# A new order of attention steps, and a PSUM tile of its own for each pair's product, in a fused fp32 attention and two-layer MLP kernel

## The chip, the core and the metric

The kernel runs on one core of a Trainium2 chip. The metric is the device time of one execution in microseconds (us); the time of a kernel is the median of several executions. Five engines work side by side, each through its own queue in order: PE (TensorE, matrix products), DVE (VectorE), ACT (ScalarE), POOL (GpSimd) and SP (SyncE, which here issues all transfers and a few relays).

## What is computed

Causal attention over 2 batches of 12 heads, 448 positions and 64 columns per head; its output, read as 896 tokens of 768 columns, goes through two blocks of two matrix products each.

```python
# attention, q, k, v of shape (2, 12, 448, 64)
scores = np.where(mask, -1e9, q @ k.T / 8)          # mask: keys later than the query
attn = exp(scores - max) / sum                      # softmax per query
x = (attn @ v), heads side by side                  # (896, 768)
# first block: 768 -> 2048 -> 768
h = x @ w_in;  x = (h * sigmoid(h)) @ w_out
# second block: 768 -> 1024 -> 768
h = x @ w_in;  s = h * softmax(h)
x = ((s - mean(s)) / sqrt(var(s) + 1e-6) * g_ln) @ w_out
```

## The kernel before

**Stages.** The attention comes first (to 84 us of the profile), then the four matrix products w1 to w4 of the two blocks. In the products every fp32 operand is split into a high and a low part of a shorter type (`xh` and `xl`, `wh` and `wl`), and three matmuls (high by high, low by high, high by low) replace one; `gemm1` (L367) is the first of them, three matmuls for each block of 128 weights. Weights arrive in chunks of 128x384 as 64-bit words, whose halves are put together on the core: `load_w` (SP), `conv_a` (ACT), `shift_w`, `sign_low` and `rest_high` (DVE; the chunk's bit steps), `split_high` (ACT) and `split_low` (POOL). After the attention `feed` (L341) does this chunk by chunk, `fed` being the next chunk to start and `pend` the chunks whose bit steps are done and whose split is due.

**Attention.** Two heads make a pair; twelve pairs, p = 0 to 11, go through the same steps. Queries of a pair come in four groups c = 0 to 3 (the last holds 64 queries of both heads), so there are seven units (j, c). The order of all steps is written out as a string, `ORDER` (L49), one word for each step; the loop at L442 walks it and each engine takes its own steps in that order. The words, with the engine and the line that a profile shows:

- `Sa` PE L155, scores of groups 2 and 0; `Sb` and `Sc` PE L165 and L155, group 3 in two passes and group 1. `f` is a relay on SP (L174) between the two passes, since both write one bank.
- `m` DVE L185, masked maximum of a unit, from PSUM into the SBUF tile `e`; `e` ACT L191, its exponential and sum; `r` DVE L197 and L198, reciprocals of a pair's seven sums; `n` the unit's scaling by the reciprocal, on POOL (L205, ending G in the word), ACT (L203, A) or DVE (L207, V).
- `T` PE L219, transposes of a half of a pair's weights into PSUM; `x` their eviction into `aT`, on ACT (L236) or DVE (L234).
- `P` PE L248, the pair's product with v; `h` its high part into `xh` on DVE (L255) or ACT (L257); `l` its low part into `xl`, DVE L262.
- `q`, `v`, `w` transfers on SP (L129, L135, L269); `ca`, `sh`, `sl`, `rh`, `sp`, `wl` the steps of a weight chunk as above (L275, L296, L280, L286, L302, L306); `g` PE, half of a `gemm1` for the first batch, whose pairs 0 to 5 are ready before the others.

**PSUM slots.** The number after a slash in a word names one of four slots; a slot is two banks, and `slot(n)` (L140) hands out a new tile in it, called `x` in the profile. A first writer of the new tile waits for the readers of the tile before it in that slot. A tile is one thing for the semaphores: a reader of it waits for the writes before it anywhere in the tile, and a writer for the reads before it anywhere in the tile. In `pv` (L240) two pairs, p and p^1, share one tile, one bank each:

```python
if n is not None:
    both = slot(n)
    pvs[p], pvs[p ^ 1] = both[:, p % 2], both[:, 1 - p % 2]
```

`scores_a` (L422) puts groups 2 and 0 of a pair into one tile as well. After the string, L449 sets `fed[0] = EARLY` (4): four chunks have been worked through by the table, and the fifth begins with `feed`.

Of the kernel before, what the change touches and what calls it, by code (L numbers as in the profile page):

```python
# [45 lines left out]

ORDER = """  # L49
Sa0/0 m0.10 m0.00 e0.00 e0.10 Sb0/1 m0.02 m0.12 e0.02 f0 Sc0 e0.12 m0.03 Sa1/2 q4 m0.01 e0.03 m0.11 Sb1/3 m1.02  # L50
e0.01 Sb2/0 f1 m1.00 Sa2/1 e0.11 m1.12 f2 v11 e1.02 m1.10 r0 Sc1 e1.00 m2.12 n0.00G e1.12 m2.10 n0.01G Sb3/2 m1.03
Sc2 e1.10 n0.10G f3 v0 m1.01 e2.12 n0.11G m1.11 v1 Sc3 m2.03 e1.01 n0.12G q5 e1.11 m2.02 Sa3/3 w0 n0.02G e1.03 m2.00
m3.11 T0.0/1 m2.01 n0.03G e2.03 r1 m2.11 e2.01 n1.01G m3.03 Sa4/0 x0.1A x0.0A n1.02G m3.01 m3.00 Sb4/2 m3.10 e2.00
n1.10G m3.02 T0.1/1 e2.11 f4 n1.12G q6 m4.00 Sc4 m3.12 x0.2A n1.00G m4.10 e3.00 m4.02 n1.11G e2.10 T1.0/3 m4.12
e2.02 n1.03G m4.03 Sb5/0 e3.02 r2 f5 q7 x0.3A x1.1V Sc5 n2.10G m4.11 v3 e3.10 n2.01G m4.01 w1 T1.1/1 e3.11 x1.0V
n2.00G w2 e3.01 Sa5/2 n2.11G v6 e4.02 x1.2V n2.02G v2 P0/3 e4.01 m5.03 w3 n2.12G e4.03 m5.12 v10 m5.01 n2.03G e3.03
m5.11 x1.3V e4.00 T2.0/0 e3.12 m5.00 Sa6/1 m5.10 e4.11 m5.02 e5.00 r3 T2.1/2 sh1 e4.10 n3.02G h0V e5.10 P1 m6.00
x2.1A m6.12 n3.12G x2.0A m6.02 e5.11 n3.01G m6.10 x2.2V e5.01 Sb6/0 n3.03G e4.12 x2.3V Sb7/1 f6 Sc6 n3.11G e5.03 h1V
f7 q8 q9 n3.00G r4 T3.1/2 e5.02 l0 q10 n4.01G Sc7 x3.2A v8 l1 n3.10G x3.3A v5 n4.12G m6.03 T3.0/3 e6.02 m6.01 Sa7/2
n4.02G e6.10 m6.11 m7.03 e5.12 n4.10G P2/0 m7.12 x3.0A n4.00G m7.00 n4.11G r5 x3.1A m7.10 e6.03 n4.03G m7.01 m7.11  # L60
e6.12 T4.0/3 m7.02 n5.01G e6.01 T4.1/1 x4.0V n5.12G x4.2A Sa8/2 e7.11 sh0 n5.11G h2V ca0 P3 x4.1V n5.00G e7.00 l2
n5.10G e6.00 n5.02G m8.00 x4.3A m8.12 e6.11 n5.03G m8.10 Sb9/3 h3V ca1 T5.0/1 f9 m8.02 e7.10 v4 Sc9 q11 l3 x5.1A
x5.0A sl0 Sb8/2 T5.1/0 e7.03 r6 f8 sl1 n6.00G Sa9/1 n6.10A m9.03 x5.3A n6.01G x5.2A Sc8 m9.01 rh0 n6.02G e7.02 m9.00
P5/0 w4 m9.10 e9.01 m8.11 ca2 m8.01 n6.11G m9.11 e7.12 n6.12G m8.03 e7.01 P4 m9.12 n6.03G h5A r7 e9.00 l5 n7.10G
e9.11 m9.02 n7.11G sp0 T6.0/3 rh1 n7.02G h4A Sb10/2 x6.0V e9.03 T6.1/1 f10 w5 n7.01A n7.00G Sc10 x6.1V v9 x6.3A
n7.12G l4 x6.2A Sb11/3 m10.11 n7.03G T7.0/0 e9.10 m10.03 f11 v7 e8.00 Sa10/1 m10.01 e9.12 wl0 x7.1V T7.1/2 e10.11
x7.0V e10.01 Sc11 sh3 x7.2A m11.03 Sa11/0 x7.3A m10.10 sh2 e9.02 m11.02 P7/2 e10.10 r9 ca3 m10.12 n9.12G e8.03
m11.01 m11.11 n9.10G e8.01 P6 sl2 n9.02G e8.11 h7V e8.12 n9.01V n9.11G m11.12 sp1 g0 e8.02 m11.00 n9.03G m10.02
e10.12 m11.10 l7 n9.00G e8.10 wl1 m10.00 e10.03 r8 T9.0/0 h6V e11.02 n8.03G T9.1/1 l6 e10.00 g1 n8.01A x9.1V n8.10G
e10.02 n8.00V n8.02V n8.12V x9.2A r10 x9.3A n8.11V n10.03G T8.0/2 x9.0V e11.11 T8.1/1 n10.12A n10.02V n10.01G e11.12  # L70
x8.0V P9/0 e11.10 n10.10G x8.3A n10.11V sl3 x8.2A rh3 e11.03 x8.1V P8 e11.01 rh2 e11.00 n10.00V w6 sp3 r11 w7
T10.0/1 h8V wl3 n11.03A T10.1/2 n11.11A l8 n11.02A g3 n11.12G h9V x10.3A x10.1V n11.00G n11.01A l9 sp2 x10.0V x10.2A
wl2 T11.1/0 n11.10A T11.0/2 x11.3V x11.0A P10/1 sh4 x11.2V x11.1A P11 h10V l10 g2 h11A ca4 l11
"""


# [669 lines left out]
```

## Time and profile before

| what | us |
|---|---|
| median of 3 runs (lowest to highest) | 434.87 (434.47 to 436.15) |
| the profiled execution, its own time | 436.2 |
| its span on the core | 434.4 |
| PE busy / DVE busy / ACT busy / POOL busy | 423.1 / 321.2 / 221.0 / 176.6 |
| first matmul of `gemm1` into tile `h`, behind the attention | at 84.02 |

The span is the stretch between the first and the last instruction; the profiled execution's own time is 1.8 us longer. A row of a timeline gives the start, the duration, the engine, the line, what is written and read with the tile names, and in brackets how long the engine sat idle before it and which engine's instruction ended that wait. [...] A PE that is shown busy may still be fed slowly in the attention, since the ends of matmuls are modelled.

### The profile page before, as it was taken

Reading aid. Unit: us, or ns where it says so; the run is one execution under the profiler, and the core shown is the slowest. Engines: PE = TensorE matmul, PEld = TensorE weight load, DVE = VectorE, ACT = ScalarE, POOL = GpSimd, SP = SyncE. Lnnn points to the kernel's source line nnn. Section 1 sums busy time; section 2 is a strip of 40 time slices with the busy share of each in tenths; the row PEclk is TensorE's granted clock in tenths of the full one; section 3 lists DMA queues with packets and bytes.
Section 4 is the critical chain, followed back from the end, with each engine's and each line's share of the span. In section 5 each row is a group of like instructions: output and inputs, shape, how many; then the busy total and the mean of one; then the engine's idle time right before and its main releaser. Section 6 shows DMA issues by size and latency. Waiting matters only on the chain.

```text
span 434.4 us, 7381 instructions
## 1 busy us (share of the span) xinstructions
PE 423.1 (97%) x2617; PEld 375.4 (86%) x2617; DVE 321.2 (74%) x696; ACT 221.0 (51%) x511; POOL 176.6 (41%) x195
## 2 busy tenths in 40 slices
PE   8988989999999999999999999999999999999996
PEld 6766667789999999999999999999888888999996
DVE  4997989599999999998695959857887877511110
ACT  4989799534344353434443434443467675612121
POOL 2977755067776777764352333333500010000000
PEclk9999999999999999999999999999999999999999
DMA  7775322034344352434664856644023310010101
GB/s 223 211 253 199 111 65 72 4 109 147 89 131 114 104 146 81 139 111 148 179 188 140 223 154 209 186 139 145 2 72 111 109 36 2 36 38 37 55 37 54
DMA packets 19764, 50.02 MB, mean 115 GB/s; under 512 B 2320, under 2 KB 4368, under 8 KB 19728
## 3 DMA queue, kind: packets, MB, share of 16 engines
q1 hardware_dynamic: 19728, 49.56, 37.1%
q8 instruction: 20, 0.33, 0.3%
q14 instruction: 16, 0.13, 0.1%
HBM read 46.80 MB, written 2.75 MB: 114 GB/s over the span
## 4 chain that ended last, share of the span: by engine, by line
PE 89%; DVE 4%; POOL 3%; DMA 1%; ACT 1%; issue 1%; SPq 0%; ACTq 0%; POOLq 0%; DVEq 0%
PE h L374 8%; PE h L373 8%; PE h L372 8%; PE h L495 7%; PE h L494 7%; PE h L493 7%; PE x L248 5%; PE ps L665 4%; PE ps L666 4%; PE ps L664 4%; PE h L611 4%; PE h L610 4%; PE h L609 4%; PE x L155 2%; PE x L219 2%; POOL e L205 2%
## 5 line engine op out<-in xcount | busy, mean ns | idle before, releaser
L306 POOL TENSOR_TENSOR wl<-wx,wh 128x384 fp32r<-128x384 f32 x64 | 79.3, 1242 | 85.9 <-ACT wh L302 76.7
L275 ACT ACTIVATE wr<-wr 128x384 f32<-128x384 f32 x96 | 52.8, 555 | 34.8 <-DMA wr<-w_in 34.4
L286 DVE SCALAR_TENSOR_TENSOR wx<-wr,wx 128x384 uint32<-128x384 uint32 x96 | 67.5, 703 | 0.1
L302 ACT ACTIVATE wh<-wx 128x384 fp32r<-128x384 f32 x64 | 33.3, 521 | 65.4 <-DVE wx L286 52.2
L374 PE MATMUL h<-xh,wl 128*128 128x448 f32 x174 | 63.2, 363 | 0.8 <-POOL wl L306 0.8
L372 PE MATMUL h<-xh,wh 128*128 128x448 f32 x174 | 63.0, 362 | 0.7 <-DVE xl L262 0.7
L373 PE MATMUL h<-xl,wh 128*128 128x448 f32 x174 | 63.1, 362 | 0.0
L296 DVE TENSOR_SCALAR wr<-wr 128x384 uint32<-128x384 uint32 x96 | 59.8, 623 | 4.2 <-DMA wr<-w_in 3.8
L280 DVE SCALAR_TENSOR_TENSOR wx<-wr 128x384 uint32<-128x384 uint32 x96 | 59.4, 619 | 1.3 <-POOL gl L382 1.3
L495 PE MATMUL h<-gh,wl 128*128 128x448 f32 x160 | 58.1, 363 | 0.0
L494 PE MATMUL h<-gl,wh 128*128 128x448 f32 x160 | 58.0, 362 | 0.0
L493 PE MATMUL h<-gh,wh 128*128 128x448 f32 x160 | 57.6, 360 | 0.0
L205 POOL TENSOR_TENSOR e<-e,st 128x384 f32<-128x384 f32 (+3 forms) x67 | 43.5, 684 | 22.8 <-DVE st L198 18.1
L382 POOL TENSOR_TENSOR gl<-sg,gh 128x448 fp32r<-128x448 f32 x32 | 41.0, 1282 | 21.4 <-DVE gh L381 10.8
L191 ACT ACTIVATE e<-e,st 128x256 f32<-128x256 f32 (+3 forms) x84 | 43.5, 524 | 5.6 <-DVE st L185 5.6
L664 PE MATMUL ps<-w4h,lh 128*128 128x384 f32 (+2 forms) x112 | 38.0, 339 | 0.0
L666 PE MATMUL ps<-w4h,ll 128*128 128x384 f32 (+2 forms) x112 | 37.5, 335 | 0.0
L665 PE MATMUL ps<-w4l,lh 128*128 128x384 f32 (+2 forms) x112 | 37.5, 335 | 0.0
L185 DVE CUSTOM_DVE_ANT_0 e<-x,mask 128x128 f32<-128x128 f32 (+3 forms) x84 | 32.7, 444 | 6.4 <-PE x L155 6.4
L653 DVE TENSOR_TENSOR ll<-tp,lh 128x512 fp32r<-128x512 f32 x14 | 9.0, 687 | 37.6 <-ACT lh L652 37.6
L372 PEld LDWEIGHTS h<-xh,wh 128*128 128x128 f32 x174 | 32.6, 187 | 3.8 <-DVE xl L262 1.0
L374 PEld LDWEIGHTS h<-xh,wl 128*128 128x128 f32 x174 | 32.6, 188 | 3.0 <-POOL wl L306 1.2
(95 smaller groups left out, 824.9 us busy)
## 6 DMA issues: line engine op xcount, KB each, us to landing
...
```

What stands on the lines that cost most here:

```text
L280: nc.vector.scalar_tensor_tensor(x.bitcast(U32), r[:, :, 1], 0x80000000, r[:, :, 0], ALU.bitwise_and, ALU.bitwise_or)
L286: nc.vector.scalar_tensor_tensor(xu, r[:, :, 1], 3, xu, ALU.logical_shift_left, ALU.bitwise_or)
L296: nc.vector.tensor_scalar(low, low, 29, None, ALU.logical_shift_right)
L306: eng.tensor_tensor(l, wx.pop((n, c)), h.bitcast(F32), ALU.subtract)
L372: nc.tensor.matmul(ps[:, :S], wh, rh, start=turn == 0 and k % NB == 0, stop=False)
L373: nc.tensor.matmul(ps[:, :S], wh, rl, start=False, stop=False)
L374: nc.tensor.matmul(ps[:, :S], wl, rh, start=False, stop=turn == 1 and k % NB == NB - 1)
L493: nc.tensor.matmul(ps[:, :S], wh, rh, start=f == 0, stop=False)
L494: nc.tensor.matmul(ps[:, :S], wh, rl, start=False, stop=False)
L495: nc.tensor.matmul(ps[:, :S], wl, rh, start=False, stop=f == KF - 1)
L664: nc.tensor.matmul(ps[:, :w], lh[:, k], w4h[:, k, ns], start=k == 0, stop=False)
L665: nc.tensor.matmul(ps[:, :w], lh[:, k], w4l[:, k, ns], start=False, stop=False)
```

## The change

The string is replaced by another of the same kind. Its words are the same, with these differences in the counts: seven of the twelve high parts `h` are on ACT instead of three; of the evictions `x.0` and `x.1` ACT has six each instead of five, of `x.2` and `x.3` seven each instead of nine, and DVE the others; five more scalings of 256 columns are on POOL, four fewer on ACT and one fewer on DVE, and one of 384 columns has gone from DVE to ACT; the fifth weight chunk's bit steps (`sl4`, `rh4`), the sixth's shift (`sh5`) and `conv_a` (`ca5`) and the ninth's transfer (`w8`) are in the table; `So` is new. In the code, `pv` takes a slot for each pair, `So` puts pair 0's group 0 into a tile of its own ahead of group 2, and after the table `fed` stands at 5 with chunk 4 pending.

```diff
 ORDER = """
-Sa0/0 m0.10 m0.00 e0.00 e0.10 Sb0/1 m0.02 m0.12 e0.02 f0 Sc0 e0.12 m0.03 Sa1/2 q4 m0.01 e0.03 m0.11 Sb1/3 m1.02
...
-wl2 T11.1/0 n11.10A T11.0/2 x11.3V x11.0A P10/1 sh4 x11.2V x11.1A P11 h10V l10 g2 h11A ca4 l11
+v3 So0/0 v0 Sa0/1 m0.10 m0.00 e0.00 e0.10 Sb0/2 m0.02 m0.12 f0 v1 Sc0 e0.12 e0.02 Sa1/3 m0.11 q4 m0.03 v7 e0.11
...
+x11.1V P11/2 w8 g3 h11V l11
 """
...
         def pv(p, n):
-            if n is not None:
-                both = slot(n)
-                pvs[p], pvs[p ^ 1] = both[:, p % 2], both[:, 1 - p % 2]
-            t = pvs[p]
+            t = pvs[p] = slot(n)[:, 0]
             v = vs[p]
...
         def scores_a(p, n):
             sa[p] = slot(n)
-            for c in (2, 0) if p else (0, 2):
+            for c in (2, 0) if p else (2,):
                 scores(p, c)
 
+        def scores_ahead(p, n):
+            sa[p] = slot(n)
+            scores(p, 0)
+
         emit = {
-            "Sa": lambda p, n, u, e: scores_a(p, n), "Sb": lambda p, n, u, e: scores_last(p, n, True),
+            "So": lambda p, n, u, e: scores_ahead(p, n), "Sa": lambda p, n, u, e: scores_a(p, n), "Sb": lambda p, n, u, e: scores_last(p, n, True),
...
-        fed[0] = EARLY
+        fed[0] = EARLY + 1
+        pend.append(EARLY)
```

What moves is shown at three places, before first and then after. The lines of the changed kernel are numbered a little differently (its L157, L221, L247, L254 and L261 are L155, L219, L248, L255 and L262 of before).

PE, the very first scores, behind five warm-up matmuls; 128x128 is group 0, 128x384 group 2, 128x224 the first pass of group 3. Before:

```order
L155 MATMUL x_139<-qk 128x128 x2
L155 MATMUL x_139<-qk 128x384 x2
L165 MATMUL x_148<-qk 128x224 x4
L155 MATMUL x_148<-qk 128x256 x2
L155 MATMUL x_161<-qk 128x384 x2
```

After:

```order
L157 MATMUL x_141<-qk 128x128 x2
L157 MATMUL x_146<-qk 128x384 x2
L167 MATMUL x_153<-qk 128x224 x4
L157 MATMUL x_153<-qk 128x256 x2
L157 MATMUL x_167<-qk 128x384 x2
```

The order is the same; groups 0 and 2, which shared the tile x_139, are now in two tiles, x_141 and x_146.

PE, the products of pairs 0 and 1 (`P0` and `P1`; the transposes between them are of later pairs). Before:

```order
L248 MATMUL x_407<-aT,v_216 64x448 x2
L248 MATMUL x_407<-aT,v_216 64x320 x2
L248 MATMUL x_407<-aT,v_216 64x192 x2
L248 MATMUL x_407<-aT,v_216 64x64 x2
L219 MATMUL x_431<-ident,e_93 128x64 x16
L155 MATMUL x_450<-qk 128x384 x2
L155 MATMUL x_450<-qk 128x128 x2
L219 MATMUL x_461<-ident,e_93 128x64 x16
L248 MATMUL x_407<-aT,v_222 64x448 x2
```

After:

```order
L247 MATMUL x_373<-aT,v_144 64x448 x2
L247 MATMUL x_373<-aT,v_144 64x320 x2
L247 MATMUL x_373<-aT,v_144 64x192 x2
L247 MATMUL x_373<-aT,v_144 64x64 x2
L221 MATMUL x_394<-ident,e_92 128x64 x16
L157 MATMUL x_414<-qk 128x384 x2
L157 MATMUL x_414<-qk 128x128 x2
L221 MATMUL x_428<-ident,e_93 128x64 x16
L221 MATMUL x_450<-ident,e_93 128x64 x16
L247 MATMUL x_470<-aT,v_159 64x448 x2
```

Pair 1's product went to the tile of pair 0, x_407; now it has one of its own, x_470, and stands one half of a pair's transposes later.

DVE, the end of the attention, to the first step of the next stage (L380, in after L379); x_1125 and x_1267 are the tiles of pairs 8 and 9, and 10 and 11, before, and x_1215 and x_1293 those of pairs 10 and 11 after. Before:

```order
L262 TENSOR_TENSOR xl<-x_1125,xh 128x448
L234 COPY aT<-x_1165 128x2x384
L234 COPY aT<-x_1229 128x8x64
L296 TENSOR_SCALAR wr<-wr 128x384
L234 COPY aT<-x_1229 128x2x256
L255 CAST xh<-x_1267 128x448
L262 TENSOR_TENSOR xl<-x_1267,xh 128x448 x2
L380 TENSOR_TENSOR sg<-ps,sg 128x448
```

After:

```order
L279 SCALAR_TENSOR_TENSOR wx<-wr 128x384
L285 SCALAR_TENSOR_TENSOR wx<-wr,wx 128x384
L236 COPY aT<-x_1232 128x2x384
L261 TENSOR_TENSOR xl<-x_1215,xh 128x448
L285 SCALAR_TENSOR_TENSOR wx<-wr,wx 128x384
L236 COPY aT<-x_1232 128x2x128
L254 CAST xh<-x_1293 128x448
L261 TENSOR_TENSOR xl<-x_1293,xh 128x448
L379 TENSOR_TENSOR sg<-ps,sg 128x448
```

Pair 10's high and low parts stood with pair 11's behind both products; pair 10's low part now stands ahead of pair 11's last eviction, and two bit steps of weight chunks stand there too. On PE, `g2` stood behind `P10` and `P11`; now `P10` stands ahead of pair 11's transposes, `g2` behind them, and `g3` behind `P11`.

## Rows read from the trace of the kernel before

**Rows 1.** Stages: us, busy (instructions) of PE, PEld, DVE, ACT, POOL; clock; DMA share, GB/s.

```profile
120.00:180.00 60.00, 60.00 (x302) 56.24 (x301) 58.85 (x88) 24.96 (x53) 43.69 (x36) 1.00 0.38 112
6.34:73.40 67.06, 61.91 (x732) 45.37 (x732) 60.65 (x239) 61.34 (x205) 44.53 (x68) 1.00 0.47 156
```

**Rows 2.** Timeline of DVE: waits of pair 2's and pair 10's tail steps.

```profile
40.95 0.62 DVE L262 TENSOR_TENSOR xl<-x,xh 128x448 fp32r<-128x448 f32 x1 [1.72 <-PE x L248]
...
81.39 0.62 DVE L255 CAST xh<-x 128x448 fp32r<-128x448 f32 x1 [2.65 <-PE x L248]
```

**Rows 3.** Timeline of PE: P1, first matmul into h, and a later wait.

```profile
27.99 1.95 PE L248 MATMUL x<-aT,v 128*64 128x448 f32 x16 [1.26 <-DVE xh L255]
...
84.02 0.47 PE L372 MATMUL h<-xh,wh 128*128 128x448 f32 x1 [0.67 <-DVE xl L262]
...
92.71 0.47 PE L374 MATMUL h<-xh,wl 128*128 128x448 f32 x1 [0.79 <-POOL wl L306]
```

**Rows 4.** Timeline of ACT: its longer waits in mid-attention.

```profile
32.24 1.09 ACT L236 ACTIVATE aT<-x 128x512 f32<-128x512 f32 x2 [1.16 <-PE x L219]
...
44.90 0.40 ACT L203 ACTIVATE e<-e,st 128x128 f32<-128x128 f32 x1 [1.15 <-DVE st L198]
...
50.27 0.55 ACT L257 ACTIVATE xh<-x 128x448 fp32r<-128x448 f32 x1 [1.38 <-PE x L248]
```

**Rows 5.** Timelines at the start: first scores, maxima, exponentials; a transfer's issue.

```profile
3.55 0.80 PE L155 MATMUL x<-qk 64*128 64x128 f32 x4
...
4.78 0.85 PE L155 MATMUL x<-qk 64*128 64x384 f32 x2
...
5.80 0.29 DVE L185 CUSTOM_DVE_ANT_0 e<-x,mask 128x128 f32<-128x128 f32 x1 [4.47 <-PE x L155]
...
6.34 0.40 ACT L191 ACTIVATE e<-e,st 128x128 f32<-128x128 f32 x1 [4.33 <-DVE st L185]
...
8.23 0.62 DVE L185 CUSTOM_DVE_ANT_0 e<-x,mask 128x448 f32<-128x448 f32 x1 [0.96 <-PE x L155]
...
13.03 0.37 SPq L129 DMA_DIRECT2D qk<-qk_in  x1
```

**Rows 6.** ACT's groups, 0 to 84 us: busy us, mean ns, idle before.

```profile
L236 ACT ACTIVATE aT<-x 128x512 f32<-128x512 f32 x18 | 9.9, 583 | 1.2 <-PE x L219 1.2
...
L236 ACT ACTIVATE aT<-x 128x768 f32<-128x768 f32 x5 | 4.0, 800 | 0.6 <-PE x L219 0.6
...
L302 ACT ACTIVATE wh<-wx 128x384 fp32r<-128x384 f32 x4 | 2.1, 516 | 0.0
L203 ACT ACTIVATE e<-e,st 128x256 f32<-128x256 f32 x4 | 2.0, 495 | 0.0
L236 ACT ACTIVATE aT<-x 128x256 f32<-128x256 f32 x5 | 1.9, 373 | 0.3 <-PE x L219 0.3
```

**Rows 7.** Timelines of ACT, POOL, DVE and PE at the attention's end.

```profile
72.50 0.19 ACT L191 ACTIVATION_READ_ACCUMULATOR e<-e,st 128x1 f32 x1
...
73.18 1.01 POOL L306 TENSOR_TENSOR wl<-wx,wh 128x384 fp32r<-128x384 f32 x1 [2.44 <-ACT wh L302]
...
75.98 0.95 DVE L234 COPY aT<-x 128x768 f32<-128x768 f32 x1
...
76.43 1.30 PE L219 MATMUL x<-ident,e 64*128 64x64 f32 x32
77.66 3.68 PE L248 MATMUL x<-aT,v 128*64 128x448 f32 x32
```

**Rows 8.** Waits of PE in the attention: total us, times, longest.

```profile
PE x L219 <- DVE st L185: 1.9, 2, 1.2
```

**Rows 9.** DVE bit steps and POOL: one step's min/median/max; two rows side by side.

```profile
L286 DVE SCALAR_TENSOR_TENSOR wx<-wr,wx x96: 541/550/1380, 46.0 to 366.7; 128x384 uint32<-128x384 uint32 x96
...
88.49 1.40 POOL L382 TENSOR_TENSOR gl<-sg,gh 128x448 fp32r<-128x448 f32 x1 [0.33 <-DVE gh L381]
...
88.80 1.31 DVE L296 TENSOR_SCALAR wr<-wr 128x384 uint32<-128x384 uint32 x1
```

More of the change, by code (lines that the diff above doesn't have):

```diff
@@ L49 @@
 ORDER = """
-Sa0/0 m0.10 m0.00 e0.00 e0.10 Sb0/1 m0.02 m0.12 e0.02 f0 Sc0 e0.12 m0.03 Sa1/2 q4 m0.01 e0.03 m0.11 Sb1/3 m1.02
[L51 to L69, printed above, removed]
@@ L70 @@
-e10.02 n8.00V n8.02V n8.12V x9.2A r10 x9.3A n8.11V n10.03G T8.0/2 x9.0V e11.11 T8.1/1 n10.12A n10.02V n10.01G e11.12
-x8.0V P9/0 e11.10 n10.10G x8.3A n10.11V sl3 x8.2A rh3 e11.03 x8.1V P8 e11.01 rh2 e11.00 n10.00V w6 sp3 r11 w7
-T10.0/1 h8V wl3 n11.03A T10.1/2 n11.11A l8 n11.02A g3 n11.12G h9V x10.3A x10.1V n11.00G n11.01A l9 sp2 x10.0V x10.2A
-wl2 T11.1/0 n11.10A T11.0/2 x11.3V x11.0A P10/1 sh4 x11.2V x11.1A P11 h10V l10 g2 h11A ca4 l11
+v3 So0/0 v0 Sa0/1 m0.10 m0.00 e0.00 e0.10 Sb0/2 m0.02 m0.12 f0 v1 Sc0 e0.12 e0.02 Sa1/3 m0.11 q4 m0.03 v7 e0.11
@@ new lines @@
+Sb1/0 v8 m0.01 e0.03 Sb2/1 m1.12 f1 Sc1 e0.01 m1.02 f2 e1.12 m1.00 Sc2 r0 q5 m1.01 e1.02 n0.10G w0 m1.10 Sa2/2
+n0.01G m1.11 e1.00 m1.03 e1.10 n0.02G Sa3/3 e1.01 m2.01 m2.12 n0.11G e1.11 Sb3/0 m2.10 e1.03 n0.03G m2.11 f3 Sc3
+m2.02 e2.10 r1 n0.12G e2.01 m2.03 q7 e2.11 n1.01G m3.00 w1 T0.1/1 m3.02 e2.02 n1.11G v2 m2.00 e2.12 m3.11 q6 Sb4/2
+n0.00G m3.12 w2 n1.10G e3.11 m3.10 n1.02G f4 v4 m3.01 e2.00 T0.0/3 m3.03 e2.03 v10 n1.03G Sc4 x0.2V v6 x0.1A x0.0A
+w3 Sa4/0 x0.3V n1.12G e3.02 r2 T1.1/3 m4.03 n2.03G q8 e3.01 v5 m4.10 P0/1 e3.10 x1.3V n1.00G e3.00 x1.2V n2.01G
@@ new lines @@
+e3.12 n2.11G m4.01 e3.03 m4.11 T1.0/3 n2.02G m4.12 h0A Sa5/2 ca0 n2.10V n2.12G m4.00 x1.0A m4.02 r3 n2.00G T2.1/0
+x1.1A sh0 e4.01 n3.12G l0 T2.0/3 e4.11 x2.2V P1/1 n3.10G x2.0A x2.3V n3.03G e4.00 m5.10 e4.02 sl0 n3.02G m5.00 x2.1A
+P2/0 m5.12 e4.10 sh1 h1A n3.01G m5.02 e4.12 l1 n3.11G e4.03 Sb5/3 h2V n3.00G T3.1/2 e5.00 f5 r4 e5.02 T3.0/1 l2
+n4.00G n4.02G Sc5 e5.10 x3.2V x3.0A x3.3V n4.03G Sa6/0 x3.1A m5.11 e5.12 sh2 n4.11G P3/2 m5.03 e5.11 m5.01 n4.12G
+ca1 m6.10 e5.01 m6.00 m6.12 n4.01G e5.03 m6.02 Sb6/1 n4.10G ca3 T4.1/3 r5 f6 q9 h3A rh0 T4.0/0 n5.10G x4.3A l3 Sc6
@@ new lines @@
+n5.00G x4.2A sl1 n5.02G x4.0A Sa7/2 m6.11 m6.03 e6.02 n5.01G m7.00 e6.11 m7.02 n5.12G x4.1A P4/3 m7.12 e7.02 n5.11G
+m7.10 m6.01 e6.12 n5.03G Sb7/0 h4V e6.03 T5.0/2 f7 l4 e7.00 T5.1/1 x5.0V e6.10 Sb8/3 e6.00 Sc7 f8 e7.10 x5.1V e6.01
+rh1 Sa8/2 m7.01 x5.3A r6 x5.2A Sc8 m7.03 n6.10G e7.01 n6.12G m7.11 e7.03 P5/1 m8.10 m8.01 n6.11G e7.12 m8.03 n6.00G
+m8.00 sp1 n6.02G m8.12 e7.11 m8.11 Sa9/0 h5A n6.01G m8.02 sp0 r7 n6.03G T6.0/3 e8.10 l5 Sb9/2 e8.12 m9.10 n7.03G
+T6.1/1 x6.1V f9 e8.00 q10 x6.0V Sc9 q11 x6.3A n7.01G w4 x6.2A m9.00 n7.12G P6/3 m9.02 e8.02 n7.02V n7.11G e8.01
@@ new lines @@
+m9.03 e8.11 m9.11 n7.10G e8.03 m9.01 T7.1/1 n7.00G m9.12 T7.0/2 e9.00 r8 x7.3A n8.11G x7.0V Sa10/0 x7.2A n8.00G
+e9.10 n8.01G Sb10/1 x7.1V e9.12 n8.02V P7/2 n8.03G f10 w5 e9.11 m10.10 h6V v9 e9.03 m10.00 n8.10G l6 e9.02 n8.12G
+m10.12 Sc10 e9.01 m10.02 wl0 h7A T8.0/3 r9 e10.12 l7 T8.1/0 n9.02G x8.0A m10.01 Sa11/2 x8.3V n9.12G x8.1A e10.02
+x8.2V P8/3 n9.11G e10.10 m10.11 ca4 n9.01G m10.03 e10.00 n9.10G m11.02 e10.01 n9.00G m11.10 Sb11/0 e10.11 n9.03G
+m11.00 m11.12 T9.0/1 e10.03 f11 h8V Sc11 wl1 e11.02 l8 T9.1/2 ca2 r10 m11.03 g0 n10.00A n10.10G x9.3A n10.11G m11.11
@@ L74 @@
+x9.2A x9.0V n10.02G n10.12A e11.12 x9.1V n10.01G P9/2 sl2 e11.03 rh2 n10.03A m11.01 w6 e11.00 sh3 ca5 T10.1/1 v11
+sh4 sh5 e11.11 T10.0/0 sp2 g1 x10.1V e11.10 wl2 x10.0V e11.01 x10.3A r11 x10.2A n11.01V n11.03G n11.02A P10/0 sl3
+h9A n11.00A n11.12A n11.11V n11.10V l9 T11.0/1 h10A sl4 T11.1/2 rh3 g2 x11.3A x11.0V w7 x11.2A l10 sp3 rh4 wl3
+x11.1V P11/2 w8 g3 h11V l11
 """
```

## The prediction

> **What bounds the kernel now.** I read the stages first [rows 1]: from 120 us on PE is busy for the whole of each stage at a full clock, while in the attention (6.34 to 73.40) no engine is full. PE's work behind the attention is the same before and after, so the time moves by what the attention and the first chunks behind it lose or gain. Dense work begins with the first matmul into `h` at 84.02, and PE has one more wait, 0.79, ended at 92.71 [rows 3]; after that none. So I need the moment of that first matmul, and whether the 0.79 stays.
>
> Within the attention three engines are about equally loaded: in the 67.06 us from the first exponential to the start of pair 11's scalings DVE works 60.65, ACT 61.34 and PE, as far as its busy time tells, 61.91 [rows 1]. None can be much shorter, and what can go is waits. Next I read those. PE stood 1.26 before P1 until DVE had read pair 0's product [rows 3]: P1 doesn't read what `h0` writes, so this is the shared tile. DVE stood 1.72 before `l2`, until P3 had written the other bank of its tile, and 2.65 before `h10`, which ended at 81.39, just when P11 ended (77.66 + 3.68 = 81.34) and not when P10 did [rows 2, 7]. ACT stood 1.16 for transposes that came late behind P1, 1.15 for the reciprocals that came late behind `l2`, and 1.38 before `h5`, whose product P5 stands ahead of P4 in their tile, until P4 had ended [rows 4].
>
> **The change, part by part.** I follow ACT to the last exponential of pair 11, since ACT's own queue grows there and DVE's shrinks a little (ahead of pair 11's scalings two high parts, five scalings, one `x.0`, one `x.1` and two merges go, six evictions of 512 columns, two shifts and one low part come).
>
> *A, up to pair 11's last exponential.* Before: it ended at 72.50 + 0.19 = 72.69 [rows 7]. ACT began at 6.34 [rows 5] and worked 61.34 less the 0.51 of one `split_high` behind it, 60.83 [rows 1]; so it waited 72.69 - 6.34 - 60.83 = 5.52. Of this 3.69 are the three waits above, 0.47 stood early (for the second pass of group 3), and 1.36 are small ones.
>
> After, ACT's work ahead of that point differs by: two `conv_a` and one `split_high` more, 3 x 0.52; three high parts more, 3 x 0.55; two `x.0` more, 2 x 0.80; two `x.1` more, 2 x 0.37; six of the 512-column evictions fewer, 6 x 0.58; two 256-column scalings fewer (0.50 each) against one of 448 (taken at 0.7) [rows 4, 6]. 1.56 + 1.65 + 1.60 + 0.75 - 3.50 - 0.30 = 1.76 more.
>
> The early tile: group 0's scores are written by 3.55 + 0.80 = 4.35, but the first maximum began only at 5.80, when group 2 was in the same tile too [rows 5]. With the handover of 0.17 that the rows show there (group 2's scores ended at 4.78 + 0.85 = 5.63) the maxima begin at 4.5 and, 0.54 later as before, the exponentials at 5.0. It brings less than these 1.3: after two exponentials ACT waits for group 2 (maxima at 5.80 as before, exponentials at 6.35), and after two more for the relayed tile, whose first maximum stands at 8.23 and doesn't move [rows 5]. That is 0.55 and about 1.1 of wait, 1.65 in place of 0.47.
>
> The shared tile's 3.69 go. The small 1.36 I keep. What comes in their place: seven more tiles pass through the four slots (54 before: 12 Sa, 12 Sb, 24 T, 6 P; now 61), and a tile's first writer waits for the last reader of the one before it. The trace has this wait of PE for DVE's maxima, 1.9 in two places before transposes [rows 8], 0.95 each. Following the queues through the new string at the prices of these rows I find slots mostly free in time, so I add one such wait less its overlap, 0.84. Waits after: 1.65 + 1.36 + 0.84 = 3.85.
>
> So the last exponential ends at 5.0 + 60.83 + 1.76 + 3.85 = 71.4: **A = 1.3**. Bounds: if all old waits come back in other places (5.52 + 1.18 at the start), 74.3, a loss of 1.6; if the small ones go too and no new one comes, 69.2, a gain of 3.5.
>
> *B, from there to dense work.* Before: 84.02 - 72.69 = 11.33, with P10 and P11 in one row (3.68) behind both transposes, then `g2`, which takes 84.02 - 0.67 - 81.34 = 2.0, and 0.67 of wait for pair 11's low part, which came behind pair 10's [rows 3, 7]. After, the chain is: six ACT steps (`x10.3`, `x10.2`, `h9` and three scalings: 2 x 0.58, 0.55, 3 x 0.5 = 3.2; P10, 1.84, runs beside them), a half of pair 11's transposes, 1.30 / 2 = 0.65, then on DVE `x11.0` 0.95, `l10` 0.62, `rh4` 0.55 and `x11.1` about 0.4 (as ACT's 0.37), then P11 1.84 and `g3` 2.0 [rows 2, 3, 4, 6, 7, 9]: 10.2. `g2` runs beside DVE's part, and `h11` and `l11` (2 x 0.62) beside `g3`, which replaces the 0.67. `g3` needs `wl3`: `x11.3`, `x11.2`, `sp3` and POOL's 1.01 [rows 7] end about 1.0 before P11 does; if that cover went, `g3` would wait. Each of the eleven rows overlaps the next by up to 0.1 (ACT's starts lie that much closer than its durations), so 9.2 to 10.2: a gain of 1.1 to 2.1. I take 1.5, **B = 1.5**.
>
> *C, the 0.79.* It ended when POOL finished chunk 4's low part. Its bit steps now stand in the attention, so `wl4` can follow POOL's `gl`, which ended at 88.49 + 1.40 = 89.89 [rows 9], and be done by 89.9 + 1.0 to 1.4 = 91.3 at the latest, where PE asks for it at 92.71 - 0.79 = 91.92. **C = 0.8**, at least 0 if the margin of 0.6 is lost. The price of the three bit steps that it adds on DVE lies in DVE's queue, which isn't the longer one.
>
> The transfers cost nothing on the path, as long as SP is through with them when a relay behind them is due: `v3`, `v0` and `v1` now stand ahead of the first relay, `q4`, `v7` and `v8` between the first and the second. An issue took 0.37 [rows 5], so three are 1.1, and there are six ahead of them from about 0.7 on, 3.4 in all, while the first relay is due when PE is through with group 3's first pass, behind 5.63. The second three have pair 1's scores beside them. If that cover is gone, group 1's scores come later by up to 1.1, and all of pair 0 with them.
>
> Sum: 1.3 + 1.5 + 0.8 = 3.6. The profiled execution took 436.2 (span 434.4), so it would take 432.6; the median lies 1.3 below it, 434.87, and gives **431.3**. All bounds together: from -0.5 (435.4) to 6.4 (428.5).
>
> [...] Five more scalings on POOL and three more bit steps on DVE meet. A DVE shift took 1.31 while a POOL instruction of 1.40 ran, and such merges take 0.55 at the median and up to 1.38 [rows 9]. [...]
>
> **The rivals.** (1) *The slots take back what the tile gave.* Four of the seven added tiles wait 0.95 each on the path: 3.8, so 435.1, no change that shows. For it: all engines are near equal, so any late reader stops PE and then everyone. Against: in before, two such waits stand against 50 reuses before transposes and scores [rows 8]. (2) *Slower: DVE is held by POOL.* In the attention 16 bit steps (13 before) stand in a time in which POOL is busy most of it (44.53 of 67.06 [rows 1], and longer now). Each that lies under a scaling costs up to 1.38 - 0.55 = 0.83 more. It decides from seven of them on: 5.8 turns 3.6 of gain into 2.2 of loss. With eight, 6.6: 437.9. Against: ACT has the longer queue, so DVE's loss counts only in part, and the merges' median is the plain 0.55. (3) *The shared tile isn't the cause*, and the waits are for data: then only B's end, C and the early tile stay, about 1.5 together, 433.4. Against: P1's wait for a tile that it doesn't read. (4) *The small waits go too*, A at its best: 434.87 - 3.5 - 1.5 - 0.8 = 429.1.
>
> **How the numbers follow.** The measurement can tell about 0.5% (2.2 us) from no change. Forecast 0.58; (4) 0.11; (1) 0.17; (3) 0.06; (2) 0.08. Faster by over 0.5%: 0.69, same (1 and 3) 0.23, slower 0.08. The range runs from 428.9, near the best of A, B and C, to 435.0, where rival 1 ends; it leaves out (2) and the tails, some 15 to 20 in 100.
>
> **What would show it.** In the profile after: no wait of a product (PE, L247) for a high part of another pair; the first maximum near 4.5 and that of group 1 still near 8.2; the last exponential near 71.4; the first matmul into `h` near 81.2 without a wait for a low part; no wait for `wl` behind it; and POOL's scalings no longer than now. I am wrong if PE's waits for maxima or evictions before transposes sum to over 3 us, if DVE's bit steps in the attention average above 0.8, or if dense work doesn't run through from its first matmul.

## The result and the profile after

The changed kernel took 429.57 us (median of 4 runs, 428.63 to 430.54), the kernel before beside it 435.34: a ratio of 0.9868, 95% interval 0.9835 to 0.9901. In a second measurement (the last of the experiments) it took 429.10 against 435.46, ratio 0.9855, interval 0.9837 to 0.9873. One of the eleven executions of before in that measurement was a slow one of 1487.94 and is left out of the 435.46. So it is 5.8 to 6.4 us faster, where 3.6 was forecast. Its profiled execution took 430.12 with a span of 428.3.

The stages of after (us, busy time and count of PE, PEld, DVE, ACT and POOL, then clock and DMA); the first line ends with pair 11's last exponential, the second runs from there to the first matmul into `h`:

```profile
5.07:69.91 64.84, 62.07 (x763) 45.89 (x760) 61.33 (x234) 62.49 (x208) 47.94 (x74) 1.00 0.48 171
69.91:79.46 9.55, 9.55 (x86) 7.01 (x86) 7.35 (x16) 6.41 (x12) 2.52 (x3) 1.00 0.31 98
```

The granted clock of TensorE is 1.00 in both, as in [rows 1]. ACT's waits up to the last exponential are 64.84 - 62.49 = 2.35; before they were 72.69 - 6.34 - 60.93 = 5.42. The timeline of ACT shows nearly all of them, and the last exponential at 69.69 + 0.22 = 69.91 (before 72.69 [rows 7]):

```profile
5.07 0.40 ACT L193 ACTIVATE e<-e,st 128x128 f32<-128x128 f32 x1 [3.06 <-DVE st L187]
...
6.87 0.61 ACT L193 ACTIVATE e<-e,st 128x384 f32<-128x384 f32 x1 [0.92 <-DVE st L187]
...
22.40 0.54 ACT L256 ACTIVATE xh<-x 128x448 fp32r<-128x448 f32 x1 [0.32 <-PE x L247]
...
25.72 0.81 ACT L238 ACTIVATE aT<-x 128x768 f32<-128x768 f32 x1 [0.39 <-PE x L221]
...
39.26 0.62 ACT L193 ACTIVATE e<-e,st 128x384 f32<-128x384 f32 x1 [0.42 <-DVE st L187]
...
69.69 0.22 ACT L193 ACTIVATION_READ_ACCUMULATOR e<-e,st 128x1 f32 x1
```

PE's waits from 4 to 82 us (in all, times, longest). No product (L247) waits for another pair's high part, the 1.26 of [rows 3] is gone, and the waits before transposes have shrunk from 1.9 [rows 8] to 0.8 + 0.6. One is new, 0.7 for a transfer:

```profile
PE x L221 <- DVE st L187: 0.8, 2, 0.5
PE x L157 <- DMA qk<-qk_in: 0.7, 1, 0.7
PE x L221 <- DVE st L199: 0.6, 1, 0.6
PE x L167 <- PE x L221: 0.3, 1, 0.3
PE x L167 <- SPq L176: 0.2, 1, 0.2
```

At the attention's end (timeline of PE) P11 stands ahead of `g3`, and the first matmul into `h` starts without any wait, 4.56 earlier than the 84.02 of [rows 3]:

```profile
75.67 1.95 PE L247 MATMUL x<-aT,v 128*64 128x448 f32 x16
77.55 0.48 PE L371 MATMUL ps<-xh,wh 128*128 128x448 f32 x1
...
79.46 0.36 PE L371 MATMUL h<-xh,wh 128*128 128x448 f32 x1
```

From there to the end of the span it is 428.3 - 79.46 = 348.8, before 434.4 - 84.02 = 350.4. So the 6.1 between the two spans are 2.8 up to the last exponential (forecast A: 1.3), 11.33 - 9.55 = 1.8 from there to dense work (B: 1.5) and 1.5 behind (C: 0.8).

### The profile page after: what moved, and what is told of

Its sections match the earlier page's. It is cut to its first block, busy times and chain, and to the rows that moved or that the text cites. A ratio compares the mean times of both kernels' runs of the same rounds, so it can differ in the third digit from the quotient of the medians.

```text
span 428.3 us, 7373 instructions
## 1 busy us (share of the span) xinstructions
PE 420.9 (98%) x2617; PEld 375.2 (88%) x2617; DVE 318.6 (74%) x692; ACT 221.0 (52%) x510; POOL 176.6 (41%) x200
## 4 chain that ended last, share of the span: by engine, by line
PE 96%; DMA 1%; SPq 1%; DVE 1%; issue 0%; ACT 0%; ACTq 0%
PE h L372 8%; PE h L371 8%; PE h L373 8%; PE h L498 8%; PE h L497 7%; PE h L499 7%; PE x L247 5%; PE ps L670 5%; PE h L613 5%; PE ps L668 5%; PE ps L669 5%; PE h L615 5%; PE h L614 4%; PE x L157 3%; PE x L221 3%; PE x L167 2%
## 5 line engine op out<-in xcount | busy, mean ns | idle before, releaser
L305 POOL TENSOR_TENSOR wl<-wx,wh 128x384 fp32r<-128x384 f32 x64 | 76.8, 1200 | 93.1 <-ACT wh L301 91.9
L285 DVE SCALAR_TENSOR_TENSOR wx<-wr,wx 128x384 uint32<-128x384 uint32 x96 | 66.6, 694 | 0.1
L207 POOL TENSOR_TENSOR e<-e,st 128x384 f32<-128x384 f32 (+3 forms) x72 | 46.2, 677 | 15.5 <-DVE st L200 8.8
L193 ACT ACTIVATE e<-e,st 128x128 f32<-128x128 f32 (+3 forms) x84 | 43.6, 524 | 4.6 <-DVE st L187 4.4
L187 DVE CUSTOM_DVE_ANT_0 e<-x,mask 128x384 f32<-128x384 f32 (+3 forms) x84 | 33.2, 444 | 5.2 <-PE x L157 5.1
```

Of the source, the lines that this page charges most:

```text
L285: nc.vector.scalar_tensor_tensor(xu, r[:, :, 1], 3, xu, ALU.logical_shift_left, ALU.bitwise_or)
L305: eng.tensor_tensor(l, wx.pop((n, c)), h.bitcast(F32), ALU.subtract)
```

## The experiments

I had two theories. Theory 1: the waits between two pairs that share a tile are lost time by themselves, and their end is the gain. Theory 2: those waits only mark places where the old table has its engines about equally late; the new order gives the gain. Later ones (3, 4) concern term C. This table has each profiled execution cut at the same three moments (us), and the median of all runs; the medians of before were 435.9 beside the first four, 435.4 beside the next four and 435.5 beside the last four.

| kernel | last exponential | first matmul into `h` | from there to the end | median | ratio, 95% interval |
|---|---|---|---|---|---|
| before | 72.69 | 84.02 | 350.4 | 434.9 to 435.9 | 1 |
| after | 69.91 | 79.46 | 348.8 | 429.57 | 0.9835 to 0.9901 |
| e1_before_apart | 68.81 | 79.03 | 349.9 | 429.83 | 0.9845 to 0.9875 |
| e2_after_shared | 70.02 | 79.66 | 348.9 | 430.64 | 0.9863 to 0.9892 |
| e3_after_nofifth | 68.62 | 78.63 | 349.1 | 429.52 | 0.9833 to 0.9862 |
| e4_after_noearly | 68.90 | 78.47 | 348.9 | 429.27 | 0.9831 to 0.9871 |
| e5_apart_h11 | 69.12 | 79.34 | 349.0 | 429.76 | 0.9844 to 0.9883 |
| e6_apart_fifth | 68.78 | 79.18 | 349.0 | 429.48 | 0.9830 to 0.9876 |
| e7_apart_early | 68.80 | 79.01 | 349.9 | 430.77 | 0.9856 to 0.9907 |
| e8_after_noscale | 68.42 | 77.98 | 348.9 | 429.02 | 0.9818 to 0.9876 |
| e9_after_convpool | 70.92 | 80.66 | 348.9 | 431.73 | 0.9903 to 0.9945 |
| e10_apart_convpool | 68.38 | 78.88 | 349.0 | 429.99 | 0.9861 to 0.9899 |
| e11_after_vlate | 69.11 | 78.65 | 348.9 | 429.50 | 0.9840 to 0.9879 |
| e12_after_again | 68.61 | 78.14 | 348.9 | 429.10 | 0.9837 to 0.9873 |

**The old table without the shared waits.** The two products stay in the two banks of one tile; a product and the reads of its partner's bank are declared independent:

```
+        def apart(late, early):
+            tc.declare_no_dep(late.ins, early.ins, reason="two banks of one tile")
...
+                    for r in reads.get(p ^ 1, ()):
+                        apart(m, r)          # in pv: each matmul m of P
...
+            for m in made.get(p ^ 1, ()):
+                apart(i, m)                  # in pv_hi and pv_lo: each read i
```

> The kernel before, its table unchanged; only the waits between the two pairs that share a tile are gone (a product no longer waits for the reads of the other pair's bank, and these reads not for the other pair's product). Theory 1 (the shared tile's waits are lost time by themselves): of the 3.69 us of waits that hang on the tile at least 3 go up to pair 11's last exponential, so that it ends near 69.5 (before 72.69), and h10 begins when P10 ends, so that the 0.67 before dense work goes too: 3.5 us faster in all, near 431.5. Theory 2 (the waits only mark places where this table has its engines about equally late, and the new order is what gives the gain): the last exponential ends at 72 or later, and the whole is 0 to 1 us faster, 434 to 435.

Measured: 6.1 us faster than before, by the medians as much as the whole change. The stage of e1_before_apart up to its last exponential, with the columns of the stages above, then ACT's waits in it, and then its dense start, in PE's timeline:

```profile
6.35:68.81 62.46, 60.35 (x724) 44.44 (x724) 59.83 (x236) 60.92 (x205) 44.35 (x67) 1.00 0.49 165
```

```profile
17.72 0.60 ACT L236 ACTIVATE aT<-x 128x512 f32<-128x512 f32 x1 [0.33 <-PE x L219]
...
31.29 1.09 ACT L236 ACTIVATE aT<-x 128x512 f32<-128x512 f32 x2 [0.35 <-PE x L219]
...
37.16 0.60 ACT L236 ACTIVATE aT<-x 128x512 f32<-128x512 f32 x1 [0.50 <-PE x L219]
...
55.57 0.40 ACT L191 ACTIVATE e<-e,st 128x128 f32<-128x128 f32 x1 [0.17 <-DVE st L185]
```

```profile
79.03 0.36 PE L385 MATMUL h<-xh,wh 128*128 128x448 f32 x1
...
87.18 0.47 PE L387 MATMUL h<-xh,wl 128*128 128x448 f32 x1 [0.38 <-POOL wl L319]
```

ACT does the same 60.9 us of work from the same start (6.35), and its waits fall from 5.42 to 62.46 - 60.92 = 1.54. That is 3.88, close to the 3.69 that the prediction counted as hanging on the tile. The 0.19 more is no sign that small waits hung on it too: 0.14 of it stands ahead of the three waits already (the eviction at 17.72 came at 17.86 in before), and small waits are left, 1.54 in all where the prediction had 1.36, though at other places. Theory 2 is out as an explanation of what the waits cost: with the order untouched their end gives A and 1.1 of B, 0.67 of it the wait for `l11`, which is no longer late.

**The new table with the shared waits put back,** as extra dependencies:

```
+                    for r in reads.pop(p ^ 1, ()):
+                        behind(m, r)         # in pv
...
+            if p ^ 1 in made:
+                behind(i, made[p ^ 1])       # in pv_hi and pv_lo
+            else:
+                reads.setdefault(p, []).append(i)
```

> The kernel after with the waits of a shared tile put back by hand: a pair's product waits for the reads of its partner that stand ahead of it in the table, a read that stands behind the partner's product waits for that product's end. By the trace of after only one of them would bind: h6 (54.90) would wait for the end of P7 (54.43 + 1.95 = 56.38), 1.5 us on DVE. Theory 1 (a wait on a nearly full engine is lost time): last exponential 1 to 1.5 us later than 69.91, and the whole 1 to 1.5 slower than after. Theory 2 (the order gives the gain, single waits of this size are taken up by slack behind them): within 0.5 us of after, last exponential by 70.4.

The one wait that was to bind did (timeline of DVE in e2_after_shared):

```profile
55.17 0.62 DVE L263 CAST xh<-x 128x448 fp32r<-128x448 f32 x1 [1.44 <-PE x L247]
```

From ACT's wait of 0.42 at 38.02 (39.26 in after, the same exponential) to the last exponential it took 32.00, in after 30.65: 1.35 for a wait of 1.44. To the first matmul into `h` it took 79.66 - 38.02 = 41.64, in after 40.20: all of the 1.44. So a wait on one of the full engines came through whole. Yet this kernel is still 5.3 faster than before: the new order meets only one of the shared waits. The two parts don't add up. Either the tile of its own or an order that goes around the shared tile takes the waits away, and both together give what each gives alone, within 1 us.

**After without the fifth chunk's steps, and without the early tile.**

```
- ... sl4 ... rh4 ... ca5 ... sh5 ... w8          (words of the table)
-        fed[0] = EARLY + 1
-        pend.append(EARLY)
+        fed[0] = EARLY
```

> The kernel after without the fifth chunk's bit steps in the attention (sl4, rh4, ca5, sh5, w8 taken out of the table, fed starts at EARLY as before). By the prediction's term C the 0.79 us wait of PE for chunk 4's low part comes back near 87 to 88, nothing before it moves by over 0.2: 0.8 slower than after. By the starts of the dense matmuls in before (1.15 between two in place of 0.20, and 0.31 for the next; then 0.40 and 0.31 at 107) 1.4 to 1.5 slower than after. If three bit steps of DVE in the attention were on the path, the first matmul into h comes up to 1.5 earlier than 79.46 and the two cancel.

```
-v3 So0/0 v0 Sa0/1 ...
+v3 v0 Sa0/1 ...
-            for c in (2, 0) if p else (2,):
+            for c in (2, 0) if p else (0, 2):
```

> The kernel after without the early tile: groups 0 and 2 of pair 0 go to one tile as in before. First exponential at 6.3 (after 5.07). Theory a (the early start is mostly waited away again, as the prediction had it): ACT then waits less for groups 2 and 1, and the last exponential ends 0.1 to 0.5 later than 69.91. Theory b (the early start is what gave more than was forecast): it ends 1.0 to 1.3 later, near 71.1, and group 1's first maximum is back near 8.2.

Neither is slower than after, though the forecast for e3_after_nofifth was 0.8 or 1.4 to 1.5 slower. In e3_after_nofifth no dense matmul starts late, though chunk 4's bit steps stand in the dense stage again: behind the first matmul into `h` it lost 349.1 - 348.8, a few tenths, not 0.8 or 1.5. Up to the last exponential one ACT step less (`ca5`, 0.58) shows: from the 0.42 wait on (38.44) 30.18 in place of 30.65. Nothing of it arrives at the first matmul into `h`: 78.63 - 38.44 = 40.19, in after 40.20. In e4_after_noearly the first exponential begins at 6.35, 1.28 later, and that same 0.42 wait comes at 38.27, between the 37.95 and 39.26 that the unchanged kernel shows in two executions. Its last exponential, at 68.90, came earlier than either theory had it, within what executions of one program differ by (below). The early tile's 1.28 bring no gain that shows, as theory a had it.

**Why `wl4` is no longer late.** The late starts of before remain in e1_before_apart (87.18 above). Two kernels ask which part of the new table removed them.

```
-... P11 h10V l10 g2 h11A ca4 l11
+... P11 h10V l10 g2 h11V ca4 l11
```

> The kernel before without the waits between two pairs of a tile (as e1_before_apart), and one letter more: pair 11's high part is copied by DVE, behind l10, and not by ACT. In e1_before_apart two dense matmuls still started 0.75 and 0.42 behind the ones before them in place of 0.20 (87.18 and 101.51), and its first sigmoid began 0.50 after the first matmul into h (79.03, 79.53), in after 0.39 before it, since there ACT loads the sigmoid's table (1.28) as soon as P11 ends. Theory 3 (this copy on ACT delays table, sigmoids, gl and so wl of chunk 4; the fifth chunk ahead isn't needed): the first sigmoid begins 0.9 earlier relative to the first matmul into h, both late starts go, and the time falls by 0.8 to 1.0 against e1_before_apart. Theory 4 (as the prediction's term C had it: wl4 is late because its bit steps come in the dense stage): the late starts stay, within 0.2 of e1_before_apart.

```
-... x11.1A P11 h10V l10 g2 h11A ca4 l11
+... x11.1A ca4 P11 sl4 rh4 ca5 sh5 w8 h10V l10 g2 h11A l11
```

> As e1_before_apart, with the fifth chunk's bit steps ahead of h10 (sl4 rh4 sh5 on DVE, ca4 and ca5 on ACT, w8 on SP) and its remaining steps as in after; pair 11's high part stays on ACT. They stand where DVE waited for P10 (0.96 in e1_before_apart; 0.55 + 0.55 + 0.35 = 1.45 of work), so h10 may come 0.5 later, beside P11. Theory 4 (term C): the two late starts (0.75, 0.42, and 0.11 each behind) go, 0.5 to 0.9 faster than e1_before_apart. Theory 3: the late sigmoid still holds wl4 back, since it follows POOL's gl; the late start near 87 becomes smaller but stays, less than 0.4 faster.

In e5_apart_h11 ACT loads the sigmoid's table at 77.65, before dense work, and its sigmoids run at 78.95 (the first matmul into `h` at 79.34). In e1_before_apart the sigmoids ran at 79.53, behind `h11` and `ca4` (timelines of ACT, e5 and then e1):

```profile
77.65 1.28 ACT L392 ACT_TABLE_LOAD   x1 [2.20 <-PE x L252]
78.95 1.14 ACT L392 ACTIVATE sg<-ps 128x448 f32<-128x448 f32 x2
```

```profile
77.23 0.55 ACT L269 ACTIVATE xh<-x 128x448 fp32r<-128x448 f32 x1 [2.53 <-PE x L252]
...
78.24 1.28 ACT L392 ACT_TABLE_LOAD   x1
79.53 0.98 ACT L392 ACTIVATE sg<-ps 128x448 f32<-128x448 f32 x2
```

Both kernels lose the two late starts (0.07 of the second is left in e5_apart_h11), and both take 349.0 behind the first matmul into `h` in place of 349.9. Theories 3 and 4 are both right in that either part is enough, and both wrong in what they forecast for the other part: under theory 4 the late starts were to stay in e5_apart_h11, under theory 3 one was to stay in e6_apart_fifth. The medians (429.76 and 429.48 against 429.83) can't tell 0.9 apart from nothing; the traces can. In e6_apart_fifth the dense work itself then waited 0.18 for `l11`, whose copy came later.

**The early tile alone in the old table.**

```
-Sa0/0 m0.10 ...
+So0/3 Sa0/0 m0.10 ...                     (with scores_ahead, as in the change)
```

> As e1_before_apart, with the early tile alone: group 0 of pair 0 has a tile of its own, first exponential near 5.07 in place of 6.35. Theory a (most of it is waited away at groups 2 and 1): the last exponential 0 to 0.4 earlier than 68.81. Theory b: 1.0 to 1.3 earlier. The kernel after without it ended its last exponential at 68.90, 1.0 before after itself, whose second group came late (0.92 of wait at 6.87, against 0.43 in e3_after_nofifth with the same start): what the transfers do at the start differs from run to run by 0.5, so that 0.5 here is not told apart from nothing.

First exponential at 5.19, last at 68.80 as without it (68.81): theory a again. Here the trace shows the early start being waited away (timeline of ACT):

```profile
8.76 0.67 ACT L191 ACTIVATE e<-e,st 128x448 f32<-128x448 f32 x1 [1.05 <-DVE st L185]
```

The median, 430.77, is no gain either.

**What POOL's scalings cost DVE.**

```
-... n0.10G ... n0.01G ... (72 words)
```

> The kernel after with POOL's 72 scalings of the exponentials left out (those of ACT and DVE stay), so part of the attention isn't normalized; POOL then has only low parts to do until the dense stage. It measures what POOL's work costs DVE: in after sign_low (128x384, two inputs) took 0.55 at the least and 0.91 on the mean of three in the attention, up to 1.30. If POOL holds DVE (the prediction's second rival): these steps all take 0.55, the shifts 0.35, and DVE's busy time up to the last exponential falls by over 1 us. If not: the same durations as in after.

DVE's groups up to 80 us (busy us, mean ns), in after and then without the scalings: the two bit steps of two inputs, the shift, and the maxima of 384 columns:

```profile
L187 DVE CUSTOM_DVE_ANT_0 e<-x,mask 128x384 f32<-128x384 f32 x24 | 12.9, 551 | 1.3 <-PE x L157 1.3
...
L279 DVE SCALAR_TENSOR_TENSOR wx<-wr 128x384 uint32<-128x384 uint32 x5 | 4.6, 917 | 0.0
...
L285 DVE SCALAR_TENSOR_TENSOR wx<-wr,wx 128x384 uint32<-128x384 uint32 x5 | 2.7, 540 | 0.0
...
L295 DVE TENSOR_SCALAR wr<-wr 128x384 uint32<-128x384 uint32 x6 | 2.1, 380 | 0.0
```

```profile
L183 DVE CUSTOM_DVE_ANT_0 e<-x,mask 128x384 f32<-128x384 f32 x24 | 12.9, 551 | 0.6 <-PE x L153 0.6
...
L275 DVE SCALAR_TENSOR_TENSOR wx<-wr 128x384 uint32<-128x384 uint32 x5 | 2.7, 549 | 0.0
...
L281 DVE SCALAR_TENSOR_TENSOR wx<-wr,wx 128x384 uint32<-128x384 uint32 x5 | 2.7, 541 | 0.0
...
L291 DVE TENSOR_SCALAR wr<-wr 128x384 uint32<-128x384 uint32 x6 | 1.9, 350 | 0.0
```

POOL does hold DVE, as the second rival said: `sign_low` takes 0.92 on the mean with the scalings and 0.55 without, the maxima, whose scores come from PSUM, 0.551 in both. `rest_high`, which has two SBUF inputs as well, took the same in both (0.540 and 0.541): in after only one of its five met a scaling of POOL (35.28, for 0.50), so these rows don't show whether POOL holds it too. The price is small, 16 steps by the difference of the groups 1.9 + 0.2 = 2.1 us, and the last exponential moved by 68.61 - 68.42 = 0.2 (against e12_after_again), less than the start alone can differ by. DVE is not what ends last.

**Two attempts to be faster than both.** ACT had the most work up to the last exponential (62.49, PE 62.07); POOL had idle time. So four of the weight scalings went from ACT to POOL:

```
-            nc.scalar.activation(high, high, AF.Copy, scale=DOWN)
+            if eng is nc.gpsimd:
+                eng.tensor_scalar(high, high, DOWN, None, ALU.mult)
+            else:
+                nc.scalar.activation(high, high, AF.Copy, scale=DOWN)
-... ca0 ... ca1 ... ca3 ... ca4 ...
+... ca0G ... ca1G ... ca3G ... ca4G ...
```

> The kernel after with four of the scalings of weight words (ca0, ca1, ca3, ca4; 0.58 each on ACT) on POOL, which has 15 us of idle time in the attention. It asks what bounds the attention once the shared waits are gone. If ACT's own work does (62.49 busy of 64.84 up to the last exponential): that moment comes 1.5 to 2.3 earlier than in after (69.91 in its profile, 68.4 to 68.6 where the second group came early), 1 to 2 us faster in all. If PE or the three engines together do: less than 0.5, and ACT shows new waits in place of the 2.3. Slower, if POOL's scalings, about 1 us later behind each of the four, come late for transposes.

> The kernel of e5_apart_h11 (the old table, no waits between the pairs of a tile, pair 11's high part on DVE), with ca0 to ca3 on POOL in place of ACT. With ACT as the bound: last exponential 1.5 to 2.3 earlier than 68.93 and the time near 428, faster than both kernels. With the engines about equal: within 0.5 of e5_apart_h11 (429.8).

The first is 2.6 slower than after on the same chip (431.73 against 429.10), the second no faster than e5_apart_h11. PE's waits from 4 to 82 us in e9_after_convpool, and POOL's group:

```profile
PE x L221 <- POOL e L207: 2.9, 4, 0.9
```

```profile
L275 POOL TENSOR_SCALAR wr<-wr 128x384 f32<-128x384 f32 x4 | 5.0, 1255 | 0.0
```

POOL takes 1.26 on the mean where ACT took 0.57 in after (0.55 to 0.58), the scalings behind come late, and four batches of transposes wait for them. POOL's idle time was not spare at these places. I found no version that beats the changed kernel.

Why freeing ACT brings nothing can be read from PE's rows. From 24.5 us to the first matmul into `h`, in before, after and e3_after_nofifth, with the columns of the stages:

```profile
24.50:84.02 59.52, 54.35 (x659) 39.13 (x653) 50.50 (x167) 49.67 (x156) 34.71 (x51) 1.00 0.33 112
24.50:79.46 54.96, 54.70 (x664) 40.68 (x665) 51.51 (x171) 50.90 (x157) 37.78 (x56) 1.00 0.28 93
24.50:78.63 54.13, 53.87 (x644) 39.83 (x640) 49.47 (x166) 49.96 (x154) 37.04 (x56) 1.00 0.26 85
```

PE stood idle for 59.52 - 54.35 = 5.17 before and for 0.26 after, where ACT has 54.96 - 50.90 = 4.06 idle and DVE 3.45. That a busy PE isn't just fed slowly is borne out by the starts: from ACT's 0.42 wait to the first matmul into `h` it takes 40.20, 40.19, 40.19 and 40.20 in after, e12_after_again, e3_after_nofifth and e4_after_noearly, although e3_after_nofifth has one step less on ACT and three fewer on DVE. So as far as these runs show, behind 24.5 us PE's own queue bounds the new table, and not ACT's, which the prediction followed.

**The start.**

```
-v3 So0/0 v0 Sa0/1 ... f0 v1 Sc0 ... q4 m0.03 v7 e0.11 Sb1/0 v8 ... f2 e1.12
+So0/0 Sa0/1 ... f0 Sc0 ... q4 m0.03 v3 v0 e0.11 Sb1/0 v1 ... f2 v7 v8 e1.12
```

> The kernel after with the transfers v3, v0 and v1, which stand ahead of the first relay, behind q4, and v7 and v8 behind the third relay. If they are what delays the first pairs' transfers (PE's 0.73 for pair 1's qk at 8.12, and the 0.92 of ACT at 6.87): no wait of PE for a transfer in the first 12 us, ACT's wait before the third exponential at 0.45 or below, group 1's first maximum at 7.0 or earlier, and the last exponential by 68.6. If the start differs from run to run by itself: waits of that kind stay, and no difference in time.

> The kernel after once more, unchanged, on the same chip as the three others. It shows how much its start differs from execution to execution: the last exponential at 69.91 again (then the other kernels' 68.4 to 68.9 are their doing), or between 68.4 and 69.9 with another wait before the third exponential (then they are not). 428.6 to 430.5.

The unchanged kernel, run again, ended its last exponential at 68.61, 1.3 earlier than in its first profile (the stage of e12_after_again, then its timeline of ACT):

```profile
5.07:68.61 63.54, 61.91 (x761) 45.74 (x760) 60.63 (x234) 62.15 (x208) 47.96 (x74) 1.00 0.49 174
```

```profile
6.81 0.61 ACT L193 ACTIVATE e<-e,st 128x384 f32<-128x384 f32 x1 [0.86 <-DVE st L187]
...
37.95 0.62 ACT L193 ACTIVATE e<-e,st 128x384 f32<-128x384 f32 x1 [0.42 <-DVE st L187]
```

All of the 1.3 lies ahead of the 0.42 wait (37.95 against 39.26); behind it both executions take 30.66 and 30.65. The first profile had PE wait 0.73 at 8.12 for pair 1's transfer, the second did not. So the start differs between executions of one program, by this transfer at least, and differences of up to 1.3 between single profiles ahead of 39 us can't be put down to an edit. The moved transfers (e11_after_vlate) show neither gain nor loss beyond that; the test is inconclusive.

## Why the prediction was right or wrong

*Where the time goes:* right. Dense work is PE's alone, the attention and the first chunks decide, and 429.57 lies in the range. The size was short by 2.2 us and more.

*The shared tile as the cause* (against rival 3): right. Its waits are gone, and taking only them away (e1_before_apart) gives 6.1 of the 5.8 to 6.4 by the medians; by the traces it lacks 0.7 of B and 1.0 of C.

*A, forecast 1.3, measured 2.8 and 4.1 in two executions* (set against one profile of before). The step that failed is "Waits after: 1.65 + 1.36 + 0.84 = 3.85". Measured: 2.35, and 63.54 - 62.15 = 1.39. Its other two terms held: ACT's work grew by 62.49 - 60.93 = 1.56 (62.15: 1.22) where 1.76 was worked out, and the first exponential begins at 5.07 (5.0). Of the waits:
- at the start 0.92 and 0.86 came, not 1.65. The first maximum of the relayed tile, said not to move from 8.23, began at 7.44 and 7.66. But it is no fixed point: six executions with the old table had it from 7.72 to 8.42.
- the added tile handovers, 0.84, show no price: PE's waits before transposes sum to 1.4 in the first profile, less than the 1.9 of before.
- the small waits, 1.36, were kept: 2.35 - 0.92 = 1.43 came in the first execution and 1.39 - 0.86 = 0.53 in the second. The fourth rival, "the small waits go too" at 429.1, came nearest to both medians with a chance of only 0.11, but its mechanism isn't shown: in the first execution the small waits stayed.

The path was wrong too behind 24.5 us. The prediction added up ACT's work and waits, but in e3_after_nofifth one ACT step less reached the last exponential and not dense work; what fell is PE's idle time, from 5.17 to 0.26.

*B, forecast 1.5, measured 1.8* (9.55; 9.53 in the second execution): right in size, and in that the wait for `l11` goes. But the chain that was added up (ACT's steps, half of pair 11's transposes, DVE's steps, P11, `g3`) isn't what takes the 9.55: PE is busy for all of it, and where the last exponential came earlier (e3_after_nofifth) the stretch grew to 78.63 - 68.62 = 10.01. So the size of 1.5 is in part luck. 1.1 of the gain is the shared tile's (e1_before_apart: 79.03 - 68.81 = 10.22), the rest the new order of `g2`, P11 and `g3`, in which PE has no gap from 70.63 on.

*C, forecast 0.8, measured 1.5.* The size was misread: a row's idle time counts from the modelled end of the matmul before it, while the starts, 0.20 apart when nothing waits, were 1.15 apart at 92.71 and 0.31 for the next. There was also a second late start that I passed over (timeline of PE, before; the row of 92.71 is in [rows 3]):

```profile
91.56 0.36 PE L373 MATMUL h<-xl,wh 128*128 128x448 f32 x1
...
93.02 0.36 PE L372 MATMUL h<-xh,wh 128*128 128x448 f32 x1
...
106.62 0.36 PE L374 MATMUL h<-xh,wl 128*128 128x448 f32 x1
107.02 0.47 PE L372 MATMUL h<-xh,wh 128*128 128x448 f32 x1
107.33 0.36 PE L373 MATMUL h<-xl,wh 128*128 128x448 f32 x1
```

With the restart behind `l11` (0.31 in place of 0.20) that is 0.95 + 0.11 + 0.20 + 0.11 + 0.11 = 1.48. The cause was half right. The fifth chunk ahead does remove it (e6_apart_fifth), but so does pair 11's high part on DVE (e5_apart_h11), which I had counted only in B. The new table, which has both, does without the fifth chunk's words (e3_after_nofifth); that `h11V` is what makes up for them there is argued from e5_apart_h11.

*The rivals.* (1), slots take back the gain: no such waits. (2), POOL holds DVE: it does, by 0.37 for a `sign_low`, not 0.83 for eight steps, and hardly any of it reaches the end. Its deciding point, seven held steps, was not reached: four of the 16 steps were held (0.96, 1.21 and 1.30 for a `sign_low`, 0.55 for a shift that took 0.36 without the scalings), and all average (4.6 + 2.7 + 2.1) / 16 = 0.59.

*The marks that were named:* no product waits for another pair's high part, yes; first maximum near 4.5, yes (4.52); group 1's at 8.2, no; last exponential near 71.4, no (69.91); first matmul into `h` near 81.2, no (79.46), without a wait, yes; no wait for `wl`, yes; POOL's scalings no longer, yes within 0.03 on the mean (0.842 for 384 columns, before 0.848; 0.953 for 448, before 0.931).

What stays open: how much of 0.3 to 0.7 between the medians of e1_before_apart (429.83) and after (429.57, 429.10) is the new order's. The traces give it 0.7 in B and 1.0 in C; the intervals overlap.
